# Two of the three split-float products of a first FFN matmul take bf16 operands

## The chip, the cores and the metric

The kernel runs on one core of one Trainium2 chip. The metric is the device time of one execution in microseconds (us). TensorE (PE) multiplies matrices, VectorE (DVE), ScalarE (ACT) and GpSimd (POOL) do elementwise work, SyncE (SP) issues the transfers. PE writes its results to PSUM; DVE and ACT read PSUM and SBUF, POOL works on SBUF.

## What is computed

```
w = softmax(weight_gen)                 # 8 x 4096 rows, 8 heads, 7 taps
x[s] = sum over 7 taps of w * x_in[s - 6 + k]   # per head, 192 columns
h = x @ w_in                            # (32768 x 192) @ (192 x 2048)
g = h * cos(h)
out = g @ w_out                         # (32768 x 2048) @ (2048 x 192)
```

The two weight matrices arrive as 64-bit floats, and the kernel turns them into float32 parts with integer steps on DVE; the rest is float32.

## The kernel before, in words

The 32768 rows are worked in 64 blocks of 512 rows. For each block POOL mixes the seven taps (`attention`, L248 to L278: seven products, L261, and seven sums, L276), giving the tile `xa`. PE transposes `xa`, so that the model dimension lies on partitions; these transposes of 64 columns (`transpose_row`, L316) are mixed into the second product's stream and land in spare columns of the accumulator `acc`.

Each float32 factor of the first product is held as two parts, a high part rounded to the fp32r format and a low part, the rest. So one product becomes three: high by high, and two corrections, high weights by low rows and low weights by high rows. `wa_hi`, `wa_lo`, `wb_hi`, `wb_lo` are the weights' parts, `x_hi` and `x_lo` the rows'. Before the change all of them are fp32r tiles. The second product does the same with `ghi` by `wo` (fp32r, 384 columns wide: high and low weights side by side) and `glo` by `wo_b` (bf16, 192 columns).

The main loop (L604 to L704) runs over 512 periods, eight for each block; a period makes 256 of the 2048 hidden columns. In PE's order a period holds:

- `ffn_in_first` (L333): three steps of two matmuls each, 64 rows by 512 columns; the two matmuls of a step take the two halves of the array's rows and run side by side. I call such a step a pair.
- `ffn_out` (L427): 8 pairs with `ghi`, a pair of transposes, 8 pairs with `glo`, for the group that lies six periods back.
- `ffn_in_second` (L348): six pairs like those of the first.

So a period has nine pairs of the first product, six of which are corrections.

For each period the elementwise chain is: ACT `act_turns` (L369, reads `h` in PSUM), DVE `dve_fraction` (L379), ACT `act_cos` (L383), DVE `dve_g` (L386), ACT `act_hi` (L393), DVE `dve_lo` (L397). `h` has three PSUM buffers, so `ffn_in_first` of a period waits for `dve_lo` of three periods earlier; `acc` has one, so a new group waits for ACT's copy of the last one (`evacuate`, L450 and L454), once every two periods. That copy carries the transposed rows along, into the SBUF tile `part`. `split` (L299) then turns a quarter of a block's transposed rows (128 by 256) into `x_hi` (ACT, L301) and `x_lo` (POOL, L303), from `part`. A split comes every second period; it is held back in the three periods after a softmax's exponential, which come once in 32 periods, so that two splits then fall into one period. The first four blocks are transposed whole and split 1024 columns at a time by ACT and DVE; the very first split reads PSUM.

The order on each engine is the order in which the code issues: line 707 and what follows tie every instruction to the one before it on its engine. In a period that has a split, ACT's order is turns, hi, cos, `x_hi`; DVE's is fraction, lo, g; then, after `dve_g`, come the second halves of the splits (`all_of(now)`). In the other periods ACT copies `acc` after cos.

The weights are split in `two_parts` (L124) as they arrive, ACT making the high part (L147), POOL the low one (L150). For `w_out` ACT makes a bf16 copy besides (L149); the function takes it as an optional argument.

Of the kernel before, what the change touches and what calls it, by code (L numbers as in the profile page):

```python
# [12 lines left out]
F32R = mybir.dt.float32r  # L13
I32 = mybir.dt.int32
U16 = mybir.dt.uint16
BF16 = mybir.dt.bfloat16
# [4 lines left out]
P = 128  # L21
# [22 lines left out]
def tile_softmax_conv_then_cos_ffn(  # L44
# [8 lines left out]
    nc = tc.nc  # L53
# [5 lines left out]
    F = w_in.shape[1]  # L59
# [4 lines left out]
    CT = R * P  # L64
# [12 lines left out]
    const = ctx.enter_context(tc.tile_pool(name="const", bufs=1))  # L77
    gpool = ctx.enter_context(tc.tile_pool(name="gpool", bufs=9))
    work = ctx.enter_context(tc.tile_pool(name="work", bufs=2))
# [3 lines left out]
    def h_banks(k):  # L83

        return ps_h.tile([P, 2, CT], F32, name="h", tag=f"h{k % 3}", bufs=1)
# [11 lines left out]


    wa_hi = const.tile([P, F], F32R, name="wa_hi")
    wa_lo = const.tile([P, F], F32R, name="wa_lo")  # L100

    wb_hi = const.tile([P, F // 2], F32R, name="wb_hi")
    wb_lo = const.tile([P, F // 2], F32R, name="wb_lo")
    wo = const.tile([P, NFC, 2 * D], F32R, name="wo")
    wo_b = const.tile([P, NFC, D], BF16, name="wo_b")

    def words(n, home="ghi"):

        if home == "ghi":
            raw = gpool.tile([P, 2 * CW], I32, name="raw", tag=home)  # L110
        elif home == "fin":
            raw = work.tile([P, R * D], I32, name="raw", tag=home)
        else:
            raw = work.tile([P, 2 * CT], I32, name="raw", tag=home)
        return raw[:, 0:2 * n]
# [8 lines left out]
    def two_parts(raw, hi, lo, half=None):  # L124
        shape = hi.shape[1:]
        n = math.prod(shape)

        def shaped(t, steps):
            t = t.rearrange("p (n s) -> p n s", s=steps)
            return t if len(shape) == 1 else t.rearrange("p (a b) s -> p a b s", b=shape[1])  # L130

        low, top = (shaped(raw, 2)[..., k] for k in range(2))
        size, bits = (shaped(t[:, 0:n], 1)[..., 0] for t in room.pop(0))
        nc.scalar.activation(out=size.bitcast(F32), in_=top.bitcast(F32), func=AF.Abs, scale=F64_SCALE)
        yield
        nc.vector.tensor_scalar(  # L136
            out=size, in0=size, scalar1=3, scalar2=None, op0=ALU.logical_shift_left)
        yield

        nc.vector.scalar_tensor_tensor(  # L140
            out=size, in0=top, scalar=-0x80000000, in1=size, op0=ALU.bitwise_and, op1=ALU.bitwise_or)
        yield

        nc.vector.scalar_tensor_tensor(  # L144
            out=bits, in0=low, scalar=29, in1=size, op0=ALU.logical_shift_right, op1=ALU.bitwise_or)
        yield
        nc.scalar.copy(out=hi, in_=bits.bitcast(F32))  # L147
        if half is not None:
            nc.scalar.copy(out=half, in_=bits.bitcast(F32))  # L149
        nc.gpsimd.tensor_tensor(out=lo, in0=bits.bitcast(F32), in1=hi.bitcast(F32), op=ALU.subtract)  # L150

    def w_in_a(c0, c1, home="ghi"):
        raw = words(c1 - c0, home)
        for n in range(2):
            nc.sync.dma_start(out=raw[n * D2:(n + 1) * D2],
                              in_=w_in[n * P:n * P + D2, c0:c1].bitcast(I32))
        return two_parts(raw, wa_hi[:, c0:c1], wa_lo[:, c0:c1])

    w_in_odd_even = w_in.rearrange("k (a n c) -> n k a c", n=2, c=P)

    def w_in_b(j):
        raw = words(CW)
        pairs = slice(j * CW // P, (j + 1) * CW // P)
        for n in range(2):
            nc.sync.dma_start(out=raw[n * D2:(n + 1) * D2].rearrange("k (a c) -> k a c", c=2 * P),
                              in_=w_in_odd_even[1 - n, D2:P, pairs, :].bitcast(I32))
        cols = slice(j * CW, (j + 1) * CW)
        return two_parts(raw, wb_hi[:, cols], wb_lo[:, cols])

    w_out_v = w_out.rearrange("(c p) d -> p c d", p=P)  # L170

# [111 lines left out]
    xT, transposed = {}, set()  # L283

    def traded(t):

        nc.sync.keepalive_nop([nc.sync.lower_ap(t)])
# [4 lines left out]
    def parts_of(b):  # L292
        if b not in xT:
            hi = work.tile([P, 2, CT], F32R, name="x_hi")
            lo = work.tile([P, 2, CT], F32R, name="x_lo")
            xT[b] = (hi, lo)
        return xT[b]

    def split(b, t, cs, eng):  # L299
        hi, lo = parts_of(b)  # L300
        nc.scalar.copy(out=hi[:, :, cs], in_=t)  # L301
        yield
        eng.tensor_tensor(  # L303
            out=lo[:, :, cs], in0=t, in1=hi[:, :, cs].bitcast(F32), op=ALU.subtract)

# [24 lines left out]
    def chunk(pair, n):  # L330
        return slice((2 * pair + n) * P, (2 * pair + n + 1) * P)

    def ffn_in_first(i, h=None):  # L333

        b, pair = divmod(i, NPAIR)
        x_hi, x_lo = xT[b]
        if h is None:
            h = h_banks(i)
        for m, (w, v) in enumerate(((wa_hi, x_lo), (wa_lo, x_hi), (wa_hi, x_hi))):
            for q in range(2):  # L340
                rs = slice(q * D2, (q + 1) * D2)
                nc.tensor.matmul(  # L342
                    h[:, q, :], lhsT=w[rs, chunk(pair, q)], rhs=v[rs, q, :],
                    start=(m == 0), stop=False, skip_group_check=True)
        hs[i] = h
        traded(h)

    def ffn_in_second(i):  # L348

        b, pair = divmod(i, NPAIR)  # L350
        x_hi, x_lo = xT[b]
        h = hs[i]
        prods = ((wa_hi, x_lo, 0), (wa_lo, x_hi, 0), (wb_hi, x_lo, 1), (wb_lo, x_hi, 1),
                 (wa_hi, x_hi, 0), (wb_hi, x_hi, 1))
        for m, (w, v, middle) in enumerate(prods):
            for q in range(2):
                rs = slice(q * D2, (q + 1) * D2)
                cs = slice(pair * P, (pair + 1) * P) if middle else chunk(pair, 1 - q)
                nc.tensor.matmul(  # L359
                    h[:, 1 - q, :], lhsT=w[rs, cs], rhs=v[rs, q ^ middle, :],  # L360
                    start=False, stop=(m == len(prods) - 1), skip_group_check=True)
# [77 lines left out]
    def evacuate(j):  # L439
# [9 lines left out]
        if WHOLE < bt < NB:  # L449
            nc.scalar.copy(out=part, in_=acc)  # L450
            r = group % R
            splits.append(split(bt, part[:, :, 2 * D:], slice(r * P, (r + 1) * P), nc.gpsimd))
        else:
            nc.scalar.copy(out=part[:, :, 0:2 * D], in_=acc[:, :, 0:2 * D])  # L454
# [70 lines left out]
    def all_of(*steps):  # L525
# [4 lines left out]

    late = [
        (-1, 1, w_in_a, (768, 1280)), (-1, 2, w_in_b, (1,)), (-1, 2, w_out_2, (0,)),
        (0, 3, w_in_a, (1280, 1792)), (0, 3, w_out_2, (1,)), (1, 4, w_out_2, (2, "part1")),
        (1, 4, w_out_2, (3, "part1")), (2, 5, w_in_a, (1792, 2048, "fin")),
        (2, 5, w_out_2, (4, "fin")), (4, 6, w_out_2, (5, "part1")), (4, 7, w_out_2, (6, "part1")),
        (5, 8, w_out_2, (7, "fin")),
# [19 lines left out]
    next(sm1)  # L556
    w_a0 = w_in_a(0, 256)
    w_b0 = w_in_b(0)
    load_rows(1)
    w_a1 = w_in_a(256, 768)  # L560
# [4 lines left out]
    def go_on(steps, n):  # L565
        for _ in range(n):
# [4 lines left out]
                      t=own_taps.rearrange("p (r h) k -> p r h k", h=H))  # L571
# [15 lines left out]
    go_on(w_a0, 3)  # L587
    go_on(w_b0, 3)
    first = split(0, tr, slice(0, CT), nc.vector)
    go_on(first, 1)  # L590
    all_of(w_a0, w_b0)
# [12 lines left out]
    for i in range(N + LAG + 1):  # L604
        b, pair = divmod(i, NPAIR)
# [22 lines left out]
        def products():  # L628
            if b < NB and pair == 0:
                assert b in transposed  # L630
            if whole is not None and j >= 0:

                ffn_out(j)
                ffn_in_first(i, whole)
            elif j >= N - HALF:
                if j == N - HALF:
                    last_half()
                return
            elif busy and EXP + 2 <= step <= EXP + 3:

                ffn_out(j, rest=False)
                ffn_in_first(i)
                ffn_out(j, rest=True)
            else:
                if i < N:
                    ffn_in_first(i, h_now if whole is None else whole)
                if j >= 0:
                    ffn_out(j)
            if i < N:
                ffn_in_second(i)  # L650
            if j in stores:
                stores.pop(j)()
            if j >= 0:
                evacuate(j)
# [15 lines left out]
        if whole is not None:  # L670
            t = work.tile([P, 2, CT], F32, name="part0", bufs=3)
            nc.scalar.copy(out=t, in_=whole)
            later.append(split(b + 1, t, slice(0, CT), nc.vector))
# [72 lines left out]
```

## Time and profile before

| | before |
|---|---|
| median of 3 runs | 2257.53 us (2256.68 to 2257.91) |
| span of the profiled execution | 2256.1 us |
| PE busy | 2203.8 us, 98% |
| DVE busy | 1922.0 us, 85% |
| ACT busy | 1886.0 us, 84% |
| POOL busy | 2001.4 us, 89% |
| PE idle in the first 200 us | 43.8 us |
| mean granted clock | 0.993 |

The profiled execution spans 2256.1 us, 1.4 us less than the median of the runs. A row of the timeline gives the start and the length in us, the engine, the line, the operation, out<-in with shapes, how often it follows itself, and in brackets the engine's idle time before it with what ended that. A row of the grouped view gives the group's busy time in us, the mean length of one in ns, and the idle time before the group. Matmuls overlap, since each is recorded from its start to the end of its results; what a step costs is read from start to start.

### The profile page before, as it was taken

What the parts mean: (1) busy time and instruction counts of PE and PEld (TensorE: products, weight loads), DVE (VectorE), ACT (ScalarE), POOL (GpSimd) and SP (SyncE); (2) the same over time, 40 slices, a digit from 0 to 9 for tenths busy, and PEclk for the clock granted to TensorE, in tenths of its full rate; (3) what the DMA queues carried; (4) which work ended last, traced back from release to release, by engine and by line L of the source; (5) the groups of instructions that cost most, each with busy time, mean ns of one, the idle gap of its engine ahead of it and who ended that gap; (6) DMA issues with size and microseconds to landing.
All of it is one profiled execution on the core that took longest, in us unless ns stands there. A gap on an engine that the chain in (4) does not pass through costs nothing.

```text
span 2256.1 us, 60616 instructions
## 1 busy us (share of the span) xinstructions
PE 2203.8 (98%) x26496; PEld 2009.9 (89%) x26496; DVE 1922.0 (85%) x1663; ACT 1886.0 (84%) x2111; POOL 2001.4 (89%) x1460
## 2 busy tenths in 40 slices
PE   4899999999999999999999999999999999999998
PEld 2788889889999889999999988899999999899887
DVE  7888888888888888888888888888888888888887
ACT  4788888888888888888888888888888888888886
POOL 7999999998998989989998998989989899899941
PEclk8899999999999999999999999999999999999999
DMA  6221121121221221221211211211211211212100
GB/s 157 57 59 43 33 59 39 46 51 34 51 50 36 49 59 26 50 59 27 58 46 31 59 44 41 51 43 42 51 48 37 58 30 47 59 26 53 33 9 22
DMA packets 25767, 105.55 MB, mean 47 GB/s; under 512 B 2734, under 2 KB 6566, under 8 KB 25502
## 3 DMA queue, kind: packets, MB, share of 16 engines
q1 hardware_dynamic: 25502, 101.67, 18.4%
q8 instruction: 208, 3.41, 0.6%
q14 instruction: 57, 0.47, 0.1%
HBM read 76.50 MB, written 25.17 MB: 45 GB/s over the span
## 4 chain that ended last, share of the span: by engine, by line
PE 94%; DVE 2%; ACT 2%; POOL 1%; issue 1%; DMA 0%; SPq 0%; POOLq 0%; DVEq 0%; ACTq 0%
PE acc L427 45%; PE h L359 31%; PE h L342 16%; PE acc L321 1%; DVE glo L397 1%; ACT part L450 1%; ACT ghi L393 1%; POOL xa L276 1%; POOL pr L261 1%; PE h L491 0%; DVE turn L379 0%; DMA xt<-in_x_dram 0%; DVE h L140 0%; DVE h L136 0%; PE h L312 0%
## 5 line engine op out<-in xcount | busy, mean ns | idle before, releaser
L379 DVE TENSOR_TENSOR turn<-h,turn 128x1024 f32<-128x1024 f32 x512 | 625.5, 1222 | 281.2 <-ACT turn L369 281.2
L427 PE MATMUL acc<-wo,ghi 64*128 64x384 f32 x8112 | 807.2, 335 | 0.3 <-ACT part L454 0.3
L427 PEld LDWEIGHTS acc<-wo,ghi 64*128 64x128 f32 x8112 | 736.7, 185 | 35.9 <-ACT part L450 3.1
L276 POOL TENSOR_TENSOR xa<-xa,pr 128x768 f32<-128x768 f32 (+1 forms) x384 | 703.0, 1831 | 0.6
L383 ACT ACTIVATE turn<-turn 128x1024 f32<-128x1024 f32 x512 | 543.4, 1061 | 188.5 <-DVE turn L379 185.1
L386 DVE SCALAR_TENSOR_TENSOR h<-h,turn 128x1024 f32<-128x1024 f32 x512 | 631.0, 1233 | 20.3 <-ACT turn L383 20.3
L397 DVE TENSOR_TENSOR glo<-h,ghi 128x1024 bf16<-128x1024 f32 x512 | 622.5, 1216 | 2.7 <-ACT ghi L393 1.7
L369 ACT ACTIVATE turn<-h 128x1024 int32<-128x1024 f32 x497 | 510.2, 1027 | 125.5 <-PE h L359 118.6
L261 POOL TENSOR_TENSOR pr<-xt,taps 128x768 f32<-128x768 f32 (+1 forms) x384 | 589.5, 1536 | 11.9
L393 ACT CAST ghi<-h 128x1024 fp32r<-128x1024 f32 x512 | 518.0, 1012 | 14.2 <-DVE h L386 14.2
L427 PE MATMUL acc<-wo_b,glo 64*128 64x192 bf16 x8112 | 431.1, 243 | 0.0
L466 POOL TENSOR_TENSOR part<-part,part 128x768 f32<-128x768 f32 x126 | 234.3, 1859 | 157.2 <-ACT part L450 130.3
L427 PEld LDWEIGHTS <-glo 64*128 64x128 bf16 x8112 | 333.5, 94 | 23.0 <-issue 11.0
L359 PE MATMUL h<-x_lo,wa_hi 64*128 64x512 f32 x1024 | 253.0, 477 | 0.7
L450 ACT COPY part<-acc 128x1024 f32<-128x1024 f32 x240 | 239.6, 998 | 3.6 <-PE acc L427 3.6
L342 PE MATMUL h<-x_lo,wa_hi 64*128 64x512 f32 x1024 | 217.3, 407 | 20.5 <-DVE t L144 14.1
L359 PE MATMUL h<-x_lo,wb_hi 64*128 64x512 f32 x1024 | 211.8, 397 | 0.0
L342 PE MATMUL h<-x_hi,wa_lo 64*128 64x512 f32 x1024 | 210.1, 392 | 1.3 <-POOL wa_lo L150 1.3
L359 PE MATMUL h<-x_hi,wa_hi 64*128 64x512 f32 x1024 | 211.1, 395 | 0.0
L342 PE MATMUL h<-x_hi,wa_hi 64*128 64x512 f32 x1024 | 210.5, 393 | 0.0
L359 PE MATMUL h<-x_hi,wb_hi 64*128 64x512 f32 x1024 | 208.6, 390 | 0.0
L359 PE MATMUL h<-x_hi,wb_lo 64*128 64x512 f32 x1024 | 208.5, 390 | 0.0
(73 smaller groups left out, 2163.3 us busy)
## 6 DMA issues: line engine op xcount, KB each, us to landing
xt<-in_x_dram SPq DMA_DIRECT2D x62, 960.0 KB, 6.8
out_dram<-fin SPq DMA_DIRECT2D x63, 384.0 KB, 3.4
taps<-in_weight_gen_dram SPq DMA_DIRECT2D x15, 448.0 KB, 4.8
raw<-in_moe_w_out_dram SPq DMA_DIRECT2D x8, 384.0 KB, 4.2
raw<-in_moe_w_in_dram SPq DMA_DIRECT2D x10, 256.0 KB, 10.8
xt<-in_x_dram SPq DMA_DIRECT2D x1, 768.0 KB, 10.5
xt<-in_x_dram SPq DMA_DIRECT2D x1, 540.0 KB, 5.5
raw<-in_moe_w_in_dram SPq DMA_DIRECT2D x4, 128.0 KB, 4.6
```

Of the source, the lines that this page charges most:

```text
L261: eng.tensor_tensor(out=dst.rearrange("p r (h g) -> p r h g", h=H), in0=xt[:, k + ra:k + rb, :].rearrange("p r (h g) -> p r h g", h=H), in ...
L276: eng.tensor_tensor(out=acc if k < K else xa, in0=acc, in1=old[:, ra:rb], op=ALU.add)
L342: nc.tensor.matmul(h[:, q, :], lhsT=w[rs, chunk(pair, q)], rhs=v[rs, q, :], start=(m == 0), stop=False, skip_group_check=True)
L359: nc.tensor.matmul(h[:, 1 - q, :], lhsT=w[rs, cs], rhs=v[rs, q ^ middle, :], start=False, stop=(m == len(prods) - 1), skip_group_check=True)
L369: nc.scalar.activation(out=t.bitcast(I32), in_=hs[i], func=AF.Identity, bias=0.25, scale=1.0)
L379: nc.vector.tensor_tensor(out=t, in0=hs[i], in1=t.bitcast(I32), op=ALU.subtract)
L383: nc.scalar.activation(out=t, in_=t, func=AF.Sin, bias=SIN_BIAS, scale=SIN_SCALE)
L386: nc.vector.scalar_tensor_tensor(out=hs[i], in0=hs[i], scalar=TWO_PI, in1=turns.pop(i), op0=ALU.mult, op1=ALU.mult)
L393: nc.scalar.copy(out=hi, in_=hs[i])
L397: nc.vector.tensor_tensor(out=lo, in0=hs.pop(i), in1=hi.bitcast(F32), op=ALU.subtract)
L427: nc.tensor.matmul(to, lhsT=g[rs, n, t * P:(t + 1) * P], rhs=w[rs, fc, :], start=(lo == 0 and c == 0 and (whole or s == 0)), stop=(lo == 1 ...
L450: nc.scalar.copy(out=part, in_=acc)
```

## The change

`wa_lo`, `wb_lo` and `x_lo` become bf16 tiles, with the writing instructions left where they are. Three bf16 tiles are new: `wa_b` and `wb_b`, written by ACT through the optional argument of `two_parts`, and `x_b`, written by a DVE copy in `split`, ahead of the low part's subtraction in program order. The corrections become `wa_b` by `x_lo` and `wa_lo` by `x_b` (and the same with `wb`); high by high stays in fp32r. The lines from L103 on move down by two, those from L304 on by four.

```
-    wa_lo = const.tile([P, F], F32R, name="wa_lo")
+    wa_lo = const.tile([P, F], BF16, name="wa_lo")
+    wa_b = const.tile([P, F], BF16, name="wa_b")
...
-        return two_parts(raw, wa_hi[:, c0:c1], wa_lo[:, c0:c1])
+        return two_parts(raw, wa_hi[:, c0:c1], wa_lo[:, c0:c1], wa_b[:, c0:c1])
...
-            lo = work.tile([P, 2, CT], F32R, name="x_lo")
-            xT[b] = (hi, lo)
+            half = work.tile([P, 2, CT], BF16, name="x_b")
+            lo = work.tile([P, 2, CT], BF16, name="x_lo")
+            xT[b] = (hi, half, lo)
...
-        hi, lo = parts_of(b)
+        hi, half, lo = parts_of(b)
         nc.scalar.copy(out=hi[:, :, cs], in_=t)
         yield
+        nc.vector.tensor_copy(out=half[:, :, cs], in_=t)
         eng.tensor_tensor(
             out=lo[:, :, cs], in0=t, in1=hi[:, :, cs].bitcast(F32), op=ALU.subtract)
...
-        for m, (w, v) in enumerate(((wa_hi, x_lo), (wa_lo, x_hi), (wa_hi, x_hi))):
+        for m, (w, v) in enumerate(((wa_b, x_lo), (wa_lo, x_b), (wa_hi, x_hi))):
...
-        prods = ((wa_hi, x_lo, 0), (wa_lo, x_hi, 0), (wb_hi, x_lo, 1), (wb_lo, x_hi, 1),
+        prods = ((wa_b, x_lo, 0), (wa_lo, x_b, 0), (wb_b, x_lo, 1), (wb_lo, x_b, 1),
                  (wa_hi, x_hi, 0), (wb_hi, x_hi, 1))
```

`wb_lo` and `wb_b` are changed and added like `wa_lo` and `wa_b`.

DVE's order in the middle of the program, before: three periods of the elementwise chain. The number behind a name is that of its buffer's allocation.

```order
L397 TENSOR_TENSOR glo_8319<-h_8189,ghi_8318 128x1024
L386 SCALAR_TENSOR_TENSOR h_8260<-h_8260,turn_8316 128x1024
L379 TENSOR_TENSOR turn_8387<-h_8325,turn_8387 128x1024
L397 TENSOR_TENSOR glo_8390<-h_8260,ghi_8389 128x1024
L386 SCALAR_TENSOR_TENSOR h_8325<-h_8325,turn_8387 128x1024
L379 TENSOR_TENSOR turn_8457<-h_8398,turn_8457 128x1024
L397 TENSOR_TENSOR glo_8460<-h_8325,ghi_8459 128x1024
```

And the same place after; `x_b` is the new bf16 tile, `part1` the SBUF copy of `acc`.

```order
L401 TENSOR_TENSOR glo_8395<-h_8264,ghi_8394 128x1024
L390 SCALAR_TENSOR_TENSOR h_8336<-h_8336,turn_8392 128x1024
L383 TENSOR_TENSOR turn_8463<-h_8401,turn_8463 128x1024
L401 TENSOR_TENSOR glo_8466<-h_8336,ghi_8465 128x1024
L390 SCALAR_TENSOR_TENSOR h_8401<-h_8401,turn_8463 128x1024
L306 CAST x_b_8050<-part1_8455 128x2x128
L383 TENSOR_TENSOR turn_8534<-h_8475,turn_8534 128x1024
L401 TENSOR_TENSOR glo_8537<-h_8401,ghi_8536 128x1024
```

The copy stands behind `dve_g` of one period and ahead of `dve_fraction` of the next, every second period; nothing else moved there.

DVE's order at the program's start, before: the last steps of two weight pieces, then the first block's low part.

```order
L136 TENSOR_SCALAR h_172<-h_172 128x512
L140 SCALAR_TENSOR_TENSOR h_172<-raw_96,h_172 128x512
L144 SCALAR_TENSOR_TENSOR t1_173<-raw_96,h_172 128x512
L303 TENSOR_TENSOR x_lo_196<-h_180,x_hi_195 128x1024
L204 TENSOR_REDUCE top_203<-taps_106 128x128
```

And after.

```order
L138 TENSOR_SCALAR h_174<-h_174 128x512
L142 SCALAR_TENSOR_TENSOR h_174<-raw_98,h_174 128x512
L146 SCALAR_TENSOR_TENSOR t1_175<-raw_98,h_174 128x512
L306 CAST x_b_198<-h_182 128x1024
L307 TENSOR_TENSOR x_lo_199<-h_182,x_hi_197 128x1024
L206 TENSOR_REDUCE top_209<-taps_108 128x128
```

The first block's copy, of 1024 elements from PSUM, stands ahead of the subtraction that makes the first `x_lo`.

More of the change, by code (lines that the diff above doesn't have):

```diff
@@ L99, in tile_softmax_conv_then_cos_ffn @@
     wa_hi = const.tile([P, F], F32R, name="wa_hi")
-    wa_lo = const.tile([P, F], F32R, name="wa_lo")
+    wa_lo = const.tile([P, F], BF16, name="wa_lo")
+    wa_b = const.tile([P, F], BF16, name="wa_b")
     wb_hi = const.tile([P, F // 2], F32R, name="wb_hi")
-    wb_lo = const.tile([P, F // 2], F32R, name="wb_lo")
+    wb_lo = const.tile([P, F // 2], BF16, name="wb_lo")
+    wb_b = const.tile([P, F // 2], BF16, name="wb_b")
     wo = const.tile([P, NFC, 2 * D], F32R, name="wo")
@@ L167, in w_in_b @@
         cols = slice(j * CW, (j + 1) * CW)
-        return two_parts(raw, wb_hi[:, cols], wb_lo[:, cols])
+        return two_parts(raw, wb_hi[:, cols], wb_lo[:, cols], wb_b[:, cols])
     w_out_v = w_out.rearrange("(c p) d -> p c d", p=P)
@@ L335, in ffn_in_first @@
         b, pair = divmod(i, NPAIR)
-        x_hi, x_lo = xT[b]
+        x_hi, x_b, x_lo = xT[b]
         if h is None:
             h = h_banks(i)
-        for m, (w, v) in enumerate(((wa_hi, x_lo), (wa_lo, x_hi), (wa_hi, x_hi))):
+        for m, (w, v) in enumerate(((wa_b, x_lo), (wa_lo, x_b), (wa_hi, x_hi))):
             for q in range(2):
@@ L350, in ffn_in_second @@
         b, pair = divmod(i, NPAIR)
-        x_hi, x_lo = xT[b]
+        x_hi, x_b, x_lo = xT[b]
         h = hs[i]
-        prods = ((wa_hi, x_lo, 0), (wa_lo, x_hi, 0), (wb_hi, x_lo, 1), (wb_lo, x_hi, 1),
+        prods = ((wa_b, x_lo, 0), (wa_lo, x_b, 0), (wb_b, x_lo, 1), (wb_lo, x_b, 1),
                  (wa_hi, x_hi, 0), (wb_hi, x_hi, 1))
```

## The prediction

> **What bounds the kernel now.** I read the page first, its busy times and its chain of waits.
>
> ```profile
> PE 2203.8 (98%) x26496; PEld 2009.9 (89%) x26496; DVE 1922.0 (85%) x1663; ACT 1886.0 (84%) x2111; POOL 2001.4 (89%) x1460
> PE 94%; DVE 2%; ACT 2%; POOL 1%; issue 1%; DMA 0%; SPq 0%; POOLq 0%; DVEq 0%; ACTq 0%
> ```
>
> PE carries the chain. But four engines are over 83% busy, so a shorter PE soon meets another one; how soon is read from one period. First PE's timeline in the steady part, one period from one `ghi` stream to the next.
>
> ```profile
> 373.41 1.57 PE L427 MATMUL acc<-wo,ghi 64*128 64x384 f32 x16
> 374.82 0.22 PE L321 MATMUL acc<-ident,xa 64*128 64x64 f32 x2
> 374.88 0.82 PE L427 MATMUL acc<-wo_b,glo 64*128 64x192 bf16 x16
> 375.48 0.48 PE L359 MATMUL h<-x_lo,wa_hi 64*128 64x512 f32 x2
> 375.80 0.39 PE L359 MATMUL h<-x_hi,wa_lo 64*128 64x512 f32 x2
> ...
> 377.66 0.52 PE L427 MATMUL acc<-wo,ghi 64*128 64x384 f32 x4
> ```
>
> The period is 377.66 - 373.41 = 4.25 us without a gap on PE. Then the same two periods on DVE and, below, ACT's copies between.
>
> ```profile
> 372.09 1.23 DVE L386 SCALAR_TENSOR_TENSOR h<-h,turn 128x1024 f32<-128x1024 f32 x1
> 373.98 1.23 DVE L379 TENSOR_TENSOR turn<-h,turn 128x1024 f32<-128x1024 f32 x1 [0.66 <-ACT turn L369]
> 375.12 1.22 DVE L397 TENSOR_TENSOR glo<-h,ghi 128x1024 bf16<-128x1024 f32 x1
> 376.33 1.23 DVE L386 SCALAR_TENSOR_TENSOR h<-h,turn 128x1024 f32<-128x1024 f32 x1
> 378.23 1.23 DVE L379 TENSOR_TENSOR turn<-h,turn 128x1024 f32<-128x1024 f32 x1 [0.66 <-ACT turn L369]
> ...
> 380.58 1.23 DVE L386 SCALAR_TENSOR_TENSOR h<-h,turn 128x1024 f32<-128x1024 f32 x1
> 382.48 1.23 DVE L379 TENSOR_TENSOR turn<-h,turn 128x1024 f32<-128x1024 f32 x1 [0.66 <-ACT turn L369]
> ```
>
> ```profile
> 375.24 1.06 ACT L383 ACTIVATE turn<-turn 128x1024 f32<-128x1024 f32 x1 [0.39 <-DVE turn L379]
> 376.20 1.00 ACT L450 COPY part<-acc 128x1024 f32<-128x1024 f32 x1
> 377.17 1.03 ACT L369 ACTIVATE turn<-h 128x1024 int32<-128x1024 f32 x1
> ```
>
> DVE idles 0.66 us in each period, ahead of the fraction, for ACT's turns. In the period that holds ACT's `acc` copy, ACT itself has no gap from cos to turns: fraction 373.98, cos 375.24, copy, turns 377.17, fraction 378.23. That stretch takes 4.25 us by ACT and DVE alone, as long as PE's period. The other stretch (378.23 to 382.48) holds a split; without its idle time DVE needs 380.58 + 1.23 - 378.23 = 3.58 us there. So two periods take 8.50 us by PE and 4.25 + 3.58 = 7.83 us by the ACT and DVE loop: a spare of 0.67 us for both together, and all of it sits where the change puts its copy.
>
> **What the change saves on PE.** `ghi` streams 8 pairs of 384 columns in 374.82 - 373.41 = 1.41 us, 0.46 ns a column; the 8 fp32r pairs from 375.80 to 377.66 take 0.2325 us each, 0.454 ns a column; bf16 `glo` (16 matmuls, first to last start 0.82 - 0.24 = 0.58 us, seven pairs) 0.083 us for 192 columns, 0.43 ns a column. Scaled, a bf16 pair of 512 columns is 0.221 us. fp32r's own two widths, 0.176 us at 384 columns and 0.2325 at 512, give 0.441 ns a column and 0.007 us fixed; if bf16 has that fixed part too, its pair is 0.007 + 512 x 0.398 ns = 0.211 us. Five pairs save 0.012 to 0.021 us each. The sixth is the step from bf16 `glo` to fp32r: from 374.88 to 375.80 lie eight `glo` pairs and that one, 0.92 - 0.66 = 0.26 us, so it saves 0.04 to 0.05 us. Together 0.10 to 0.155 us; I take 0.11 a period, nearer to plain scaling, 56 us over 512 if PE stays the bound. The page "TensorE: Matmul & The Clock Gate" of the Trainium skill, in its section on the back-to-back issue gap, gives 215.7 ns for 512 bf16 columns; by it the saving would be some 0.125 us a period, 64 us.
>
> **What the change adds: the copy of the rows.** These POOL and DVE rows are from the grouped view, by shape; the fourth gives the number of splits.
>
> ```profile
> L276 POOL TENSOR_TENSOR xa<-xa,pr 128x768 f32<-128x768 f32 x378 | 699.5, 1850 | 0.5
> L261 POOL TENSOR_TENSOR pr<-xt,taps 128x768 f32<-128x768 f32 x378 | 586.4, 1552 | 11.9
> L466 POOL TENSOR_TENSOR part<-part,part 128x768 f32<-128x768 f32 x126 | 234.3, 1859 | 157.2 <-ACT part L450 130.3 <-ACT part L454 26.9
> L303 POOL TENSOR_TENSOR x_lo<-part,x_hi 128x256 fp32r<-128x256 f32 x240 | 177.1, 741 | 30.5 <-ACT x_hi L301 30.3
> L467 POOL TENSOR_TENSOR fin<-part 128x384 f32<-128x384 f32 x126 | 127.6, 1013 | 9.9
> ```
>
> So 240 copies of 128x256 come onto DVE, from SBUF to SBUF. No such copy is in the trace. Its nearest kin is a one-input operation in SBUF, L217; and the few DVE operations with both inputs in SBUF (L303) show what happens beside POOL. DVE, POOL, DVE, POOL, then L217's lengths.
>
> ```profile
> 72.04 1.68 DVE L303 TENSOR_TENSOR x_lo<-part,x_hi 128x1024 fp32r<-128x1024 f32 x1
> ...
> 74.74 0.46 DVE L217 TENSOR_SCALAR den<-den 128x128 f32<-128x128 f32 x1
> ```
>
> ```profile
> 71.63 0.99 POOL L150 TENSOR_TENSOR wo<-t,wo 128x384 fp32r<-128x384 f32 x1
> 72.59 2.52 POOL L261 TENSOR_TENSOR pr<-xt,taps 128x768 f32<-128x768 f32 x1
> ```
>
> ```profile
> 115.10 1.62 DVE L303 TENSOR_TENSOR x_lo<-part,x_hi 128x1024 fp32r<-128x1024 f32 x1
> ```
>
> ```profile
> 113.79 1.85 POOL L276 TENSOR_TENSOR xa<-xa,pr 128x768 f32<-128x768 f32 x1
> 115.59 2.82 POOL L466 TENSOR_TENSOR part<-part,part 128x768 f32<-128x768 f32 x1
> ```
>
> ```profile
> L217 DVE TENSOR_SCALAR den<-den x3: 181/196/456, 5.0 to 74.7; 128x32 f32<-128x32 f32 x1, 128x64 f32<-128x64 f32 x1, 128x128 f32<-128x128 f32 x1
> ```
>
> The first L303 ends 1.09 us after POOL's L150 ended (73.72 against 72.62), the second 1.08 us after POOL's L276 (116.72 against 115.64): each stood until POOL's running instruction was over. And POOL's next one took 2.52 in place of 1.55 us, 2.82 in place of 1.86: it stood in turn. DVE and POOL exclude each other there, whole instructions long. L217 shows that one input is enough: 32 and 64 elements took 181 and 196 ns, 0.47 ns an element, two elements a DVE cycle; 128 should take 226 ns, and took 456, ending 0.09 us after POOL's L261 (75.20 against 75.11). I expect the same of the copy: 0.29 us alone, and beside POOL the rest of POOL's instruction, W, and 0.15 us (0.09 + 128 x 0.47 ns).
>
> Two pages of the Trainium skill bear on that. "VectorE: DVE Perf Modes", in its perf-mode tier table, gives a float32 copy in SBUF the doubled rate, and "SBUF — State Buffer", in the section on SBUF's two sides, says that an operation at that rate and a GpSimd one take turns on a port pair, the loser standing for the other's whole instruction. The rows above agree, L217 for the doubled rate; that a copy into bf16 does it too no row here shows, and these pages make me surer of it.
>
> What W will be: the request comes when `dve_g` ends. Three such ends, and the POOL instruction running then (two lie in the rows of DVE above, at 373.32 and 381.81; the third is here).
>
> ```profile
> 389.07 1.23 DVE L386 SCALAR_TENSOR_TENSOR h<-h,turn 128x1024 f32<-128x1024 f32 x1
> ```
>
> ```profile
> 372.05 1.85 POOL L276 TENSOR_TENSOR xa<-xa,pr 128x768 f32<-128x768 f32 x1
> ...
> 380.78 1.84 POOL L276 TENSOR_TENSOR xa<-xa,pr 128x768 f32<-128x768 f32 x1
> ...
> 390.17 1.56 POOL L261 TENSOR_TENSOR pr<-xt,taps 128x768 f32<-128x768 f32 x1
> ```
>
> W would be 0.58, 0.81 and 1.43 us, 0.94 in the mean. A request at a random moment waits for half of what runs, weighted by busy time: the five POOL groups give (699.5 x 1.85 + 586.4 x 1.55 + 234.3 x 1.86 + 177.1 x 0.74 + 127.6 x 1.01) / 2 / 2256 = 0.64 us. The phases will move, so I take 0.75, with 0.47 and 1.0 as ends.
>
> Who waits for the copy: `dve_fraction` behind it, then cos, ACT's `acc` copy and the next turns, which had no spare. The loop's two periods become 4.25 + 3.58 + W + 0.15 + 0.05 that I allow for the handoff = 8.03 + W, 8.78 us at W = 0.75, against 8.50 now: PE no longer sets the pace, and its saving is not seen. From W = 0.47 on the change loses. 225 of the pairs of periods have a copy: 0.28 x 225 = 63 us. In 15 of them two copies stand together, and the second meets the POOL instruction that has just been let go: about 1.7 + 0.15 us each, 28 us. POOL, 89% busy, loses at most some 0.1 us at each copy, 24 us, out of the idle time that the longer periods give it.
>
> **Smaller terms.** At the start:
>
> ```profile
> 20.89 0.42 DVE L144 SCALAR_TENSOR_TENSOR t<-raw,h 128x256 int32<-128x256 int32 x1
> ...
> 23.42 1.22 DVE L303 TENSOR_TENSOR x_lo<-h,x_hi 128x1024 fp32r<-128x1024 f32 x1
> ...
> 24.78 0.79 PE L342 MATMUL h<-x_lo,wa_hi 64*128 64x512 f32 x2 [2.71 <-ACT h L134]
> ```
>
> ```profile
> L147 ACT CAST wa_hi<-t 128x512 fp32r<-128x512 f32 x3 | 1.8, 612 | 3.1 <-DVE t L144 3.1
> ```
>
> The first block's copy reads PSUM; priced by the 1.22 us of L303 at that size it makes the first `x_lo`, and PE's first pair at 24.78, 1.2 us later. ACT's seven casts of weights cost up to 0.61 us each, 4 us, beside POOL's subtractions of the same pieces; I count 1 us, and 4 if nothing hides them. The three whole blocks add a copy of 1024 elements each, 0.65 us by L217's slope, or some 1.4 with W, partly in DVE's waits for ACT: 2 us. That makes 4 us, from 2 to 9. POOL's subtraction writes 2-byte elements in place of 4; I take its 741 ns as unchanged, its own wait being for `x_hi`. In the periods without copies PE's saving stays where PE is the bound, some 30 of them: 3 us.
>
> **The sum.** 2256.1 + 63 + 28 + 4 - 3 = 2348 us for the span; the median of the runs was 1.4 us above it, so 2350 us.
>
> **Rivals.**
>
> *The copy does not take turns with POOL* (it runs at one element a cycle, 0.42 us by L144, or POOL lets it in). Then the loop needs 4.25 + 3.58 + 0.42 + 0.05 = 8.30 us for two periods, or with 0.29 us 8.17, and PE 8.50 - 2 x 0.11 = 8.28. PE is about the bound: 0.20 to 0.22 x 225 = 45 to 50 us less, 2257.5 - 47 - 3 + 4 = 2212 us, from 2195 (0.155 us saved a period) to 2225. For it: no copy of this kind is in the trace, and L217's long length is a single one. Against: both L303 rows stood, and the lengthened POOL rows fit. Chance 0.17.
>
> *The lock holds, but the requests fall well* (W near 0.45): two periods take 8.48 us, the doubles find DVE ahead, and the time is 2253 to 2262 us. For it: W depends on phases that the change itself moves, and 0.58 is one of the three. Against: the other two, and the random mean of 0.64. Chance 0.06.
>
> *bf16 brings PE nothing* (its pairs stay at 0.2325 us). With the lock it changes nothing, as PE is not the bound; without it the time is 2257 to 2266 us. The bf16 rows of `glo` speak against it. Chance 0.02.
>
> **How the numbers follow.** The forecast, slower with W between 0.47 and above 1.0, has 0.75. At W = 1.0 two periods take 9.03 us: 0.53 x 225 = 119, with the doubles and the start 2257.5 + 119 + 28 + 4 - 3 = 2405 us; at 0.5 it is 0.03 x 225 = 7, so 2294, and less where the doubles are hidden. The range, 2235 to 2415 us, holds the forecast and the second and third cases but for some 0.03 above; it leaves out the first rival, 0.17. A measurement of this kernel tells about 0.2% from no change, 4.5 us. Faster by more than that: 0.17, the first rival. Within it: 0.07, the second rival and half of the third. Slower: 0.76, the forecast and the other half.
>
> **What would show it.** In the profile after: L306's copies of 128x256 far over 0.29 us in the mean, near 0.9, each ending about 0.1 us behind a POOL instruction; DVE's idle time ahead of L383 (the fraction) much under 281 us; PE with idle time ahead of the first pairs of a period or ahead of `acc`, where it now has none; bf16 pairs at 0.21 to 0.22 us. If the copies take 0.3 or 0.42 us flat, the lock is wrong and the first rival holds. If they wait as forecast and the time still falls, the loop's stretch of 4.25 us had spare that I did not see.

## The result and the profile after

The change takes 2278.25 us (median, 2277.02 to 2280.45) against 2257.11, four runs of each: 1.0094 times as long, interval 1.0080 to 1.0109. It is slower, as forecast, but by 21 us and not by 93. The range of 2235 to 2415 us holds it, near its low end.

The page after: the engines' busy times, and the chain of waits by engine.

```profile
PE 2176.8 (96%) x26496; PEld 1667.5 (73%) x26496; DVE 2084.6 (92%) x1907; ACT 1873.9 (82%) x2118; POOL 2012.0 (88%) x1460
PE 58%; DVE 27%; ACT 11%; issue 3%; POOL 0%; DMA 0%; ACTq 0%; SPq 0%; DVEq 0%; POOLq 0%
```

PE's share of the chain fell from 94% to 58%, and DVE and ACT took most of what it lost: the loop of the two now sets part of the pace. DVE is 163 us busier. The grouped view says with what. (Its rows sum to more, since a record on DVE can overlap the next one by about 0.09 us.)

```profile
L307 DVE TENSOR_TENSOR x_lo<-part,x_hi 128x1024 bf16<-128x1024 f32 x3 | 8.0, 2650 | 0.0
L306 DVE CAST x_b<-part 128x256 bf16<-128x256 f32 x240 | 188.0, 788 | 0.0
L306 DVE CAST x_b<-part 128x1024 bf16<-128x1024 f32 x3 | 3.6, 1206 | 0.0
```

The 240 copies took 0.79 us each in the mean. One that is not disturbed takes 0.28 us, as the next rows show. An instruction that waits, already started in the profile, for another engine's to end is said here, as in the prediction, to stand for it. This is DVE over two periods and a copy at each end.

```profile
542.89 0.28 DVE L306 CAST x_b<-part 128x256 bf16<-128x256 f32 x1
543.50 1.23 DVE L383 TENSOR_TENSOR turn<-h,turn 128x1024 f32<-128x1024 f32 x1 [0.33 <-ACT turn L373]
...
547.68 1.23 DVE L383 TENSOR_TENSOR turn<-h,turn 128x1024 f32<-128x1024 f32 x1 [0.60 <-ACT turn L373]
548.82 1.21 DVE L401 TENSOR_TENSOR glo<-h,ghi 128x1024 bf16<-128x1024 f32 x1
550.03 1.23 DVE L390 SCALAR_TENSOR_TENSOR h<-h,turn 128x1024 f32<-128x1024 f32 x1
551.17 0.98 DVE L306 CAST x_b<-part 128x256 bf16<-128x256 f32 x1
552.08 1.21 DVE L383 TENSOR_TENSOR turn<-h,turn 128x1024 f32<-128x1024 f32 x1
...
556.24 1.23 DVE L383 TENSOR_TENSOR turn<-h,turn 128x1024 f32<-128x1024 f32 x1 [0.60 <-ACT turn L373]
```

And POOL beside them.

```profile
542.91 1.67 POOL L263 TENSOR_TENSOR pr<-xt,taps 128x768 f32<-128x768 f32 x1
...
550.16 1.84 POOL L278 TENSOR_TENSOR xa<-xa,pr 128x768 f32<-128x768 f32 x1
551.96 0.79 POOL L307 TENSOR_TENSOR x_lo<-part,x_hi 128x256 bf16<-128x256 f32 x1
```

The first copy began 0.02 us ahead of a POOL instruction and had the way free; that POOL instruction took 1.67 us in place of 1.55. The second began while POOL's L278 ran to 552.00, and ended at 552.15: 0.15 us behind it, the figure of the forecast. Of the 240 copies 183 end 0.15 to 0.16 us behind a POOL instruction, and 57 ran free in 0.28 us. So the copy is W + 0.15 us as written, W being the rest of POOL's instruction: 0.64 us in the mean of all.

What the loop makes of it is in the fraction's starts. From 547.68 to 552.08, with a copy of 0.98 us, lie 4.40 us, so 3.42 us without it; the forecast had 3.58 + 0.05. From 552.08 to 556.24 lie 4.16 us, and from 543.50 to 547.68, behind the short copy, 4.18, where it had 4.25. ACT's rows of that second stretch:

```profile
553.32 1.06 ACT L387 ACTIVATE turn<-turn 128x1024 f32<-128x1024 f32 x1 [0.69 <-DVE turn L383]
554.28 0.99 ACT L454 COPY part<-acc 128x1024 f32<-128x1024 f32 x1
555.18 1.03 ACT L373 ACTIVATE turn<-h 128x1024 int32<-128x1024 f32 x1
...
557.50 1.06 ACT L387 ACTIVATE turn<-turn 128x1024 f32<-128x1024 f32 x1 [0.39 <-DVE turn L383]
```

The turns start 0.90 us behind ACT's copy, where the trace before had 0.97 (376.20 to 377.17): there they waited for PE as well, by a hair, and ACT looked as if it could do no better. PE's last pair for that `h`, in the trace before:

```profile
376.73 0.39 PE L359 MATMUL h<-x_hi,wb_hi 64*128 64x512 f32 x2
```

It ends at 377.12, 0.05 us ahead of the turns. So two periods are 4.18 + 3.41 + copy = 7.59 + copy by DVE and ACT (3.41 by the experiment with the copy alone, below: 549.42 - 544.36 - 1.65), and where the copy is short PE's pace holds them.

PE's own rate, from its timeline: bf16 pairs of 512 columns, 0.216 us from start to start, and no loss where bf16 and fp32r meet.

```profile
553.30 0.38 PE L363 MATMUL h<-x_lo,wa_b 64*128 64x512 bf16 x2
553.51 0.38 PE L363 MATMUL h<-x_b,wa_lo 64*128 64x512 bf16 x2
553.73 0.38 PE L363 MATMUL h<-x_lo,wb_b 64*128 64x512 bf16 x2
553.94 0.38 PE L363 MATMUL h<-x_b,wb_lo 64*128 64x512 bf16 x2
553.97 0.58 PE L363 MATMUL h<-x_hi,wa_hi 64*128 64x512 f32 x2
554.39 0.40 PE L363 MATMUL h<-x_hi,wb_hi 64*128 64x512 f32 x2
```

From 553.94 to 554.39 a bf16 and an fp32r pair take 0.45 us, the sum of their own rates. (The fp32r pair is recorded from 553.97, with a longer length; why, no run shows.)

Where the 21 us lie: DVE's turns (L375 before, L379 after) run once in 32 periods, so their first and last starts cut each span in three.

```profile
L375 DVE TENSOR_SCALAR turn<-h x15: 1224/1225/1226, 184.6 to 2096.5; 128x1024 int32<-128x1024 f32 x15
```

```profile
L379 DVE TENSOR_SCALAR turn<-h x15: 1209/1210/1211, 196.8 to 2120.6; 128x1024 int32<-128x1024 f32 x15
```

The start takes 196.8 in place of 184.6 us, 12.2 more; the middle, 14 times 32 periods, 1923.8 in place of 1911.9, 11.9 more; the end 156.6 in place of 159.6, 3.0 less. The whole gain and loss of the steady part is 0.85 us in 32 periods, where 6 had been forecast.

That is the difference of two larger ones, by the fraction's starts in the mean of these 14 cycles. The 20 periods that lie off an exponential take 83.3 us in place of 84.9, 1.6 less, though their copies stand for POOL too; halfway between two exponentials a pair of periods takes 8.31 us in place of 8.49. The twelve around it, from five before to six behind, take 54.1 us in place of 51.6, 2.5 more. Of that, 1.7 us is the period with two copies (5.70 against 4.01); the period in which DVE also takes the softmax's maximum (5.00 against 4.47) and the one after its reciprocal (4.80 against 4.14) add 0.5 and 0.7. The change gains in the ordinary periods, and loses mostly where DVE has more to do.

### The profile page after: what moved, and what is told of

The parts are those of the page before. It is cut to its first block, busy times and chain, and to the rows that moved or that the text cites. A ratio compares the mean times of both kernels' runs of the same rounds, so it can differ in the third digit from the quotient of the medians.

```text
span 2277.2 us, 60747 instructions
## 1 busy us (share of the span) xinstructions
PE 2176.8 (96%) x26496; PEld 1667.5 (73%) x26496; DVE 2084.6 (92%) x1907; ACT 1873.9 (82%) x2118; POOL 2012.0 (88%) x1460
## 4 chain that ended last, share of the span: by engine, by line
PE 58%; DVE 27%; ACT 11%; issue 3%; POOL 0%; DMA 0%; ACTq 0%; SPq 0%; DVEq 0%; POOLq 0%
PE acc L431 29%; PE h L363 19%; PE h L346 10%; DVE turn L383 9%; DVE glo L401 6%; DVE h L390 5%; ACT turn L373 4%; DVE x_b L306 3%; ACT part L454 3%; ACT turn L387 1%; ACT L387 1%; ACT L211 1%; PE acc L325 1%; ACT ghi L397 1%; DVE top L206 1%
## 5 line engine op out<-in xcount | busy, mean ns | idle before, releaser
L431 PE MATMUL acc<-wo,ghi 64*128 64x384 f32 x8112 | 815.5, 339 | 1.8 <-ACT part L458 0.4
L431 PEld LDWEIGHTS acc<-wo,ghi 64*128 64x128 f32 x8112 | 723.6, 186 | 72.0 <-ACT part L454 44.5
L278 POOL TENSOR_TENSOR xa<-xa,pr 128x768 f32<-128x768 f32 (+1 forms) x384 | 701.3, 1826 | 0.6
L263 POOL TENSOR_TENSOR pr<-xt,taps 128x768 f32<-128x768 f32 (+1 forms) x384 | 595.2, 1551 | 11.9
L431 PE MATMUL acc<-wo_b,glo 64*128 64x192 bf16 x8112 | 425.5, 243 | 0.0
L431 PEld LDWEIGHTS <-glo 64*128 64x128 bf16 x8112 | 327.5, 94 | 29.1 <-issue 12.0
L346 PE MATMUL h<-x_hi,wa_hi 64*128 64x512 f32 x1024 | 299.8, 582 | 0.0
L363 PE MATMUL h<-x_hi,wa_hi 64*128 64x512 f32 x1024 | 299.6, 581 | 0.0
L346 PE MATMUL h<-x_lo,wa_b 64*128 64x512 bf16 x1024 | 201.3, 389 | 65.4 <-DVE glo L401 44.5
L307 POOL TENSOR_TENSOR x_lo<-part,x_hi 128x256 bf16<-128x256 f32 x240 | 181.6, 759 | 30.1 <-ACT x_hi L304 30.1
L346 PEld LDWEIGHTS <-wa_b 64*128 64x128 bf16 x1024 | 49.4, 93 | 212.3 <-issue 105.9
L346 PE MATMUL h<-x_b,wa_lo 64*128 64x512 bf16 x1024 | 196.1, 379 | 1.6 <-POOL wa_lo L152 1.6
L363 PE MATMUL h<-x_lo,wa_b 64*128 64x512 bf16 x1024 | 195.8, 379 | 0.7
```

Source lines behind the costliest of these rows:

```text
L263: eng.tensor_tensor(out=dst.rearrange("p r (h g) -> p r h g", h=H), in0=xt[:, k + ra:k + rb, :].rearrange("p r (h g) -> p r h g", h=H), in ...
L278: eng.tensor_tensor(out=acc if k < K else xa, in0=acc, in1=old[:, ra:rb], op=ALU.add)
L346: nc.tensor.matmul(h[:, q, :], lhsT=w[rs, chunk(pair, q)], rhs=v[rs, q, :], start=(m == 0), stop=False, skip_group_check=True)
L363: nc.tensor.matmul(h[:, 1 - q, :], lhsT=w[rs, cs], rhs=v[rs, q ^ middle, :], start=False, stop=(m == len(prods) - 1), skip_group_check=True)
L431: nc.tensor.matmul(to, lhsT=g[rs, n, t * P:(t + 1) * P], rhs=w[rs, fc, :], start=(lo == 0 and c == 0 and (whole or s == 0)), stop=(lo == 1 ...
```

## The experiments

Every kernel is timed against the kernel before on the same chip. The theory at first: the price is DVE's standing for POOL's running instruction, the gain is PE's bf16 rate, and both show in the stretch from one fraction to the next. Rivals: DVE's extra work as such; mixed products that slow PE; weight casts at the start. Lines that are left out of a code cut are marked by three dots.

**The copy on another engine.**

```
-        nc.vector.tensor_copy(out=half[:, :, cs], in_=t)
+        nc.scalar.copy(out=half[:, :, cs], in_=t)
```

> The change with one word altered: ACT writes the bf16 copy of the rows, not DVE. Theory (DVE's copy costs what it does because it stands for POOL's running instruction): DVE has 240 copies less, ACT 240 of 0.39 us more. ACT's stretch from fraction to fraction grows from 3.6 to about 3.9 us in the periods with a split, still under PE's 4.12, so PE sets the pace again: two periods take 8.25 us in place of 8.50, about 2200 us (2190 to 2215). Rival A (it is the sheer extra work on the elementwise loop, 0.39 us here, more than DVE's 0.28): no better than the change, 2270 to 2290 us. Rival B (mixing bf16 and fp32r steps slows PE): 2255 us or more.

Measured 2220.15 us, 0.9836 (0.9821 to 0.9850). ACT's copy took 0.40 us, more than DVE's 0.28 alone, and the kernel is 37 us faster than before and 58 faster than the change. The fraction's starts, in the steady part:

```profile
631.75 1.23 DVE L383 TENSOR_TENSOR turn<-h,turn 128x1024 f32<-128x1024 f32 x1 [0.49 <-ACT turn L373]
...
635.92 1.23 DVE L383 TENSOR_TENSOR turn<-h,turn 128x1024 f32<-128x1024 f32 x1 [0.59 <-ACT turn L373]
...
640.00 1.23 DVE L383 TENSOR_TENSOR turn<-h,turn 128x1024 f32<-128x1024 f32 x1 [0.50 <-ACT turn L373]
```

```profile
L306 ACT CAST x_b<-part 128x256 bf16<-128x256 f32 x240 | 94.8, 401 | 0.0
```

Two periods take 8.25 us, the expected figure. Rival B falls, and rival A as it was put; but the copy left DVE altogether, and whether the work on DVE as such costs is for the next run to tell. The time came out 5 us above the range's upper end: the twelve periods around an exponential take 51.4 us in place of 51.6, while the 20 others go from 84.9 to 82.6. The estimate had given all of them the gain.

**The same engine and place, at one element a cycle.**

```
-        nc.vector.tensor_copy(out=half[:, :, cs], in_=t)
+        nc.vector.tensor_reduce(out=half[:, :, cs], in_=t.unsqueeze(3), axis=AX.X, op=ALU.max)
```

> The change with DVE's copy written as a maximum over one element, which DVE works at one element a cycle (its rows in the profile before: 896 elements in 1.07 us). Engine and place stay. Theory: an operation with one input in SBUF at the single rate does not stand for POOL; 128x256 take a flat 0.42 us, the DVE stretch 3.40 + 0.42 = 3.82 us stays under PE's 4.12, and the time is about 2205 us (2195 to 2220), though DVE works longer at each copy. Rival A (DVE's own work at that place is what costs): 0.14 us more at each copy than the change's 0.28, 2278 or more. Rival C (any DVE operation on SBUF stands for POOL): lengths as in the change, about 2285 us.

Measured 2226.29 us, 0.9863 (0.9848 to 0.9877), 6 us above the range.

```profile
L306 DVE TENSOR_REDUCE x_b<-part 128x256 bf16<-128x256 f32 x240 | 97.0, 409 | 0.0
```

All 240 took 0.41 us. Work that takes 0.41 us and never stands for POOL beats work that alone takes 0.28 and does, by 52 us. This is the cleanest pair of the study: engine, place and data are the same. Rivals A and C fall. (The edit holds for the first four blocks' copies too: of the 52 us, 7.5 lie ahead of DVE's first turns, which start at 189.3 in place of 196.8.)

**The copy alone**, in the kernel before: the tile `x_b` and the copy, with all products left in fp32r.

```
+            half = work.tile([P, 2, CT], BF16, name="x_b", bufs=1)
...
+        nc.vector.tensor_copy(out=half[:, :, cs], in_=t)
```

> The kernel before with DVE's bf16 copies of the rows added and read by nobody; all products stay fp32r (the copy has one buffer). Theory: the copy alone is a loss that the bf16 products then pay back in part. With PE at 8.50 us for two periods the copies over about 0.8 us show: some 3.3 us in 32 periods, 50 us over the kernel, and some 8 at the start, about 2310 us (2290 to 2330). Rival B (the products slow PE): 2257 to 2265 us.

Measured 2335.24 us, 1.0345 (1.0327 to 1.0362): 78 us slower and 5 us above the range. Rival B falls: the copy loses without any bf16 product. DVE's rows around two copies:

```profile
544.36 1.23 DVE L381 TENSOR_TENSOR turn<-h,turn 128x1024 f32<-128x1024 f32 x1 [0.66 <-ACT turn L371]
547.85 1.65 DVE L304 CAST x_b<-part 128x256 bf16<-128x256 f32 x1
549.42 1.21 DVE L381 TENSOR_TENSOR turn<-h,turn 128x1024 f32<-128x1024 f32 x1
...
553.58 1.23 DVE L381 TENSOR_TENSOR turn<-h,turn 128x1024 f32<-128x1024 f32 x1 [0.59 <-ACT turn L371]
```

```profile
L304 DVE CAST x_b<-part 128x256 bf16<-128x256 f32 x240 | 236.6, 991 | 0.0
```

544.36 to 553.58 is 9.22 us with a copy of 1.65: 7.57 + copy, the same loop. The copies are longer here, 0.99 us in the mean against 0.79: they meet POOL's instructions at other points than in the change. That this follows from PE's slower pace is likely, but no run shows it. So the bf16 products give 57 us back, in part by PE's rate and in part by shorter copies; these two are not told apart.

**The low rows alone in bf16**: `wa_b` and `wb_b` by a bf16 `x_lo`, `wa_lo` and `wb_lo` by `x_hi` in fp32r as before, no copy of the rows.

```
...
+        for m, (w, v) in enumerate(((wa_b, x_lo), (wa_lo, x_hi), (wa_hi, x_hi))):
...
```

> One part of the change alone: only the products with the low rows (wa_b and wb_b by x_lo) in bf16, low weights by x_hi stay fp32r, and no copy of the rows is made. Theory: nothing is added to DVE in the steady part; three of nine pairs in a period save 0.017 us each and the step from glo some 0.04, together 0.08 to 0.09 us a period, so about 2217 us (2210 to 2230). Rival B (mixed steps slow PE): 2255 us or more.

Measured 2231.76 us, 0.9888 (0.9873 to 0.9902). A gain without the copy, so rival B falls, but 2 us outside the range. PE's rows show most of the miss:

```profile
1000.95 0.39 PE L361 MATMUL h<-x_lo,wb_b 64*128 64x512 bf16 x2
1000.99 0.58 PE L361 MATMUL h<-x_hi,wb_lo 64*128 64x512 f32 x2
1001.41 0.39 PE L361 MATMUL h<-x_hi,wa_hi 64*128 64x512 f32 x2
```

A single bf16 pair with an fp32r one takes 0.46 us, against 0.465 for two fp32r pairs: between fp32r pairs it saves about 0.005 to 0.01 us, not the 0.017 that it saves in a row of bf16 pairs. Halfway between two exponentials a period is 0.064 us shorter than before, where 0.08 to 0.09 had been expected.

**The copy in the other stretch**, one period ahead, where ACT needs 4.18 us and DVE 3.41.

```
-        nc.vector.tensor_copy(out=half[:, :, cs], in_=t)
+        if eng is nc.vector:
+            nc.vector.tensor_copy(out=half[:, :, cs], in_=t)
...
             nc.scalar.copy(out=part, in_=acc)
             r = group % R
+            cs = slice(r * P, (r + 1) * P)
+            nc.vector.tensor_copy(out=parts_of(bt)[1][:, :, cs], in_=part[:, :, 2 * D:])
```

> The change with DVE's copy of a split moved one period ahead, right behind ACT's copy of acc, so into the other stretch, where ACT needs 4.18 us from fraction to fraction and DVE 3.41. The copies still stand for POOL, about 0.6 to 0.9 us each in the mean. Theory (what counts is the length of the stretch in which the copy stands): up to 0.77 us of a copy is free there, and as the split's own stretch shrinks to some 3.6 us, two periods stay at PE's 8.27 us for every copy up to 1.25 us; about 2232 us (2222 to 2245). Rival D (each microsecond that DVE stands for POOL is paid, wherever): 2265 to 2290 us.

Measured 2306.28 us, 1.0220 (1.0203 to 1.0238), slower than the change. This expectation failed; rival D's number was nearer, though the time lies 16 us above it too. Its rows of DVE, POOL and ACT:

```profile
641.09 1.79 DVE L458 CAST x_b<-part 128x256 bf16<-128x256 f32 x1
642.81 1.21 DVE L384 TENSOR_TENSOR turn<-h,turn 128x1024 f32<-128x1024 f32 x1
...
646.36 1.23 DVE L384 TENSOR_TENSOR turn<-h,turn 128x1024 f32<-128x1024 f32 x1
```

```profile
640.89 1.85 POOL L473 TENSOR_TENSOR part<-part,part 128x768 f32<-128x768 f32 x1 [0.58 <-ACT part L455]
```

```profile
639.82 0.99 ACT L455 COPY part<-acc 128x1024 f32<-128x1024 f32 x1
```

```profile
L458 DVE CAST x_b<-part 128x256 bf16<-128x256 f32 x240 | 294.8, 1228 | 10.4 <-ACT part L455 10.4
```

The split's own stretch did shrink, to 3.55 us (642.81 to 646.36). But ACT's copy of `acc` releases POOL's L473 too, which had been waiting, at 640.89; DVE's copy comes 0.2 us later, behind `dve_g`, and stands for all of it. Of the 240 copies 102 stand for L473, 1.80 us in the mean; the others stand for less or not at all. The copies grew to 1.23 us in the mean, and those of 1.8 us are over the 1.31 that were free (8.27 - 3.55 - 3.41). The length of a copy had been taken as a property of the copy; it is one of the place.

**The start.** The whole blocks' copies on ACT, the steady ones on DVE as in the change.

```
-        nc.vector.tensor_copy(out=half[:, :, cs], in_=t)
+        (nc.scalar.copy if eng is nc.vector else nc.vector.tensor_copy)(out=half[:, :, cs], in_=t)
```

> The change with only the first four, whole blocks' bf16 copies made by ACT; the 240 in the steady part stay on DVE. Theory: the start loses some 7 of its 11.6 us by DVE standing for POOL twice in each whole block (the copy and, behind it, the low part), so about 2271 us (2267 to 2274). Rival E (the start's loss is ACT's seven casts of weights): no gain, 2276 us or more.

Measured 2271.31 us, 1.0063 (1.0048 to 1.0078), 7 us under the change, as expected; rival E falls for these 7 us. In the change's trace a whole block stands twice, DVE first and then POOL's rows:

```profile
72.97 1.04 DVE L306 CAST x_b<-part 128x1024 bf16<-128x1024 f32 x1
73.93 2.56 DVE L307 TENSOR_TENSOR x_lo<-part,x_hi 128x1024 bf16<-128x1024 f32 x1
```

```profile
72.44 1.01 POOL L152 TENSOR_TENSOR wo<-t,wo 128x384 fp32r<-128x384 f32 x1
73.41 2.00 POOL L263 TENSOR_TENSOR pr<-xt,taps 128x768 f32<-128x768 f32 x1
75.37 2.81 POOL L278 TENSOR_TENSOR xa<-xa,pr 128x768 f32<-128x768 f32 x1
```

The copy stands for L152; when it is done POOL's next instruction goes first, and the subtraction stands for that one: 2.65 us in the mean where it took 1.52 before.

**Both moves.**

```
-        nc.vector.tensor_copy(out=half[:, :, cs], in_=t)
+        if eng is nc.vector:
+            nc.scalar.copy(out=half[:, :, cs], in_=t)
...
+            nc.vector.tensor_copy(out=parts_of(bt)[1][:, :, cs], in_=part[:, :, 2 * D:])
```

> Both moves together: the steady copies in the other stretch, the whole blocks' on ACT. Theory: the two gains add, about 2224 us (2215 to 2238). Rival D: 2258 us or more.

Measured 2298.21 us, 1.0182 (1.0167 to 1.0197). It is 8 us under the kernel with the steady copies in the other stretch, so the gain at the start adds; but it lies 60 us above the expected range, since the steady part loses as it did there. Rival D's 2258 us or more fits.

**The other place, without the standing.** After that failure the theory was mended: place and wait are two things. The same kernel with the steady copies at one element a cycle:

```
-            nc.vector.tensor_copy(out=parts_of(bt)[1][:, :, cs], in_=part[:, :, 2 * D:])
+            nc.vector.tensor_reduce(out=parts_of(bt)[1][:, :, cs], in_=part[:, :, 2 * D:].unsqueeze(3), axis=AX.X, op=ALU.max)
```

> The kernel of both moves (steady copies behind ACT's copy of acc, whole blocks' copies on ACT) with one instruction altered: the steady copies are written at one element a cycle, as a maximum over one element. Theory (the place was right, and what failed there is that POOL starts on the same ACT copy just ahead of DVE, so that DVE stands for a whole POOL instruction nearly every time): with no standing a copy is 0.41 us, the stretch 3.41 + 0.41 = 3.82 us stays under ACT's 4.18, PE sets the pace with 8.27 us for two periods, about 2218 us (2210 to 2225). Rival F (the place itself costs, by holding up the fraction ahead of the next acc copy): near 2298 us, at least over 2260.

Measured 2221.01 us, 0.9838 (0.9824 to 0.9851): 77 us less than the kernel before it, by one instruction's rate, and inside the range. The place costs nothing where the copy does not stand; rival F falls. This and the copy on ACT are level, 36 and 37 us faster than the kernel before the change, and the best that was run.

## Why the prediction was right in kind and wrong in size

**Right.** That the copy stands for POOL, and for how long (W + 0.15 us); that DVE's idle time ahead of the fraction falls (281 to 157 us); that PE then waits where it had not (44.5 us in the waits on `dve_lo`); the bf16 rate (two periods 8.25 to 8.27 us, by the forecast 8.28); what two copies in one period cost (below). The first rival's number, 2212 us without the standing, is close to the 2220 and 2226 us of the experiments that took the standing away.

**Right by luck.** The change is slower, as forecast, but not by the term that carried the forecast, the 63 us of the 225 pairs of periods. The steady part loses by the doubled copies and in two more periods of 32 and gains in most of the ordinary ones; the start adds the rest.

**The step that failed** is the loop's length, "4.25 + 3.58 + W + 0.15 + 0.05 that I allow for the handoff = 8.03 + W". Measured it is 4.18 + 3.41 + W + 0.15 = 7.74 + W. Three readings were too long. The 4.25 of ACT's stretch was PE's period seen through ACT, which happened to come free at the same moment. The 3.58 ended at the recorded end of `dve_g`, though DVE's next instruction starts about 0.09 us ahead of that end (551.17 against 550.03 + 1.23). And a handoff of 0.05 was added where the same overlap takes 0.08 away. Together 0.29 us in every one of 225 pairs of periods: at the forecast's own W of 0.75 the pair becomes 8.49 us, 0.01 under today's, and the term of 63 us becomes about -2. That alone brings the sum to 2285 us. The prediction's last sentence had named the sign of this, a stretch of 4.25 us with spare that it did not see.

**"PE no longer sets the pace, and its saving is not seen"** fell with it. A pair of periods whose copy is under 0.68 us (8.27, PE's two periods with the copy on ACT, less 7.59) goes at PE's new pace, and 142 of the 240 copies are that short.

**Terms.** Two copies in one period: forecast 1.85 us for the second, behind the POOL instruction that has just been let go. In 9 of the 15 such periods it is so. DVE, then POOL:

```profile
1314.41 2.13 DVE L306 CAST x_b<-part 128x256 bf16<-128x256 f32 x2
```

```profile
1312.92 1.54 POOL L263 TENSOR_TENSOR pr<-xt,taps 128x768 f32<-128x768 f32 x1
1314.43 1.97 POOL L278 TENSOR_TENSOR xa<-xa,pr 128x768 f32<-128x768 f32 x1
```

The first copy ran free in 0.28 us, POOL's L278 started beside it, and the second stood for all of that: 2.13 us for the two. In four others the first stood, for 1.94 to 1.98 us, and the second met the split's own subtraction, 0.81 us. Such a period grew by 1.70 us in the mean (4.01 to 5.70), 25 us in 15; the forecast's 28, and 0.28 x 15 for the first copies, make 32.

The start cost 12 us, not 4; 7 of it are the whole blocks' double standing, of which only the first was counted. What the other 5 consist of was not tried; the casts of weights may have a part in it. W, taken as 0.75, was 0.64, and 0.84 where PE kept its old pace; no rule for it came out of the runs, only that it differs with PE's pace and with the place. One W for all pairs hid the spread: the copies took from 0.28 to 1.98 us.

## What to carry to other kernels

Before work goes onto DVE beside a busy POOL, ask at which rate it runs: a copy at two elements a cycle that stands for POOL's instructions can cost three times its length (0.79 against 0.28 us here), and one at a single element a cycle, or on ACT, can be cheaper in the kernel though longer by itself. The wait belongs to the place, so look at what POOL starts just ahead of it, and at which event lets both go. When a loop of two engines is said to have no spare, take its length from starts, in a stretch where nothing else could have held it; an engine that comes free just as the bound arrives shows the bound's period, not its own.

## What the runs showed of the hardware

- DVE's copy from float32 to bf16 in SBUF, 128x256: 0.28 us alone, 0.79 us in the mean beside POOL (0.99 and 1.23 us in two other kernels). A maximum over one element of the same data: 0.41 us, beside POOL too. The page "SBUF — State Buffer" of the Trainium skill, in its section on SBUF's two sides, names the doubled rate as one of two things that make DVE and GpSimd exclude each other, two inputs in SBUF being the other; these two rows agree with the first.
- A copy of 128x256 that stands ends 0.15 us behind POOL's instruction, where alone it takes 0.28 us from its start.
- Between two DVE instructions that both stand, POOL's waiting instruction goes first: in a whole block the copy ends at 74.01, POOL's L263, recorded from 73.41, goes next and ends at 75.41, and the subtraction ends at 76.49.
- A bf16 pair of 512 columns streams in 0.216 us, an fp32r pair in about 0.233. In rows of several, a change between the types costs nothing (0.45 us for one of each); alone among fp32r pairs, a bf16 pair saves about half of that difference (0.46 against 0.465 us for two).
